# Moving the first two pairs' kv work, turns and numerator on the queues of a fused linear-attention and feed-forward kernel

## The chip, the cores and the metric

The kernel runs on one core of a Trainium2 chip. The metric is the device time of one execution in microseconds (us), median of three runs.

## The reference

A linear attention with a feature map, followed by a feed-forward layer with a leaky activation whose slope is learnt per column:

```python
def phi(x):                                   # x: [8, 8, 576, 64], w_phi: [64, 128]
    proj = np.einsum('bhsd,df->bhsf', x, w_phi)
    proj = proj - np.max(np.abs(proj), axis=-1, keepdims=True)
    return np.concatenate([np.exp(proj), np.exp(-proj)], axis=-1)
q_p, k_p = phi(q), phi(k)
kv  = np.einsum('bhsf,bhsd->bhfd', k_p, v)
z   = np.sum(k_p, axis=2)
num = np.einsum('bhsf,bhfd->bhsd', q_p, kv)
den = np.einsum('bhsf,bhf->bhs', q_p, z)[..., None] + 1e-06
x   = (num / den).transpose(0, 2, 1, 3).reshape(4608, 512)
h   = x @ w_in                                # w_in: [512, 2048]
g   = np.maximum(h, 0.0) + alpha * np.minimum(h, 0.0)
out = g @ w_out                               # w_out: [2048, 512]
```

## The kernel before

The attention runs over 32 pairs of heads (`NPAIR`, numbered from 0). For each pair these steps exist, each a small function in `attention_units(i)`:

- `load`, `load_v`: SyncE (SP) fetches k and q (tile `raw`, two buffers) and v.
- `project(0)` and `project(1)`: TensorE multiplies `raw` by `w_phi`. `project(0)` makes the four full k tiles (`pj`, 8 matmuls, the first burst); `project(1)` makes the last, half-filled k tile together with the last q tile (`pl`, 2 matmuls) and the four full q tiles (`pj`, 8 matmuls, the second burst). VectorE (DVE) then takes the largest absolute value (`m`, L320) and subtracts it (`t`, L321). From pair 2 on both bursts share one buffer of PSUM (`ps_pj`), so the second burst waits until DVE has read the first.
- `k_exp`: ScalarE (ACT) takes the two exponentials of the k tiles (`xk` for the four full ones, `k` for the last). The exponential of the last tile stands after the whole of `project(1)`, and waits until DVE has written all of its `t`.
- `k_z` (z, L374) and `k_acc` (kv, L357): matmuls into the tile `kv`, the z part first; the last quarter of each needs the `k` exponential. `kv_out` copies it (`ks`, ACT), `kv_turn` transposes it (`kt`, L389, TensorE), `kv_copy` copies that (`sf`, ACT).
- `q_turn` transposes the q tiles (`qt`, L400 and L403), `q_exp` takes their exponentials (`qf`, ACT); `den` and `num` (`d`, `n`) are the matmuls of denominator and numerator; then come the division by way of DRAM and the store of x.

Between these steps the weights of the feed-forward layer are unpacked in blocks of 256 columns: SP loads a block (`raww`), ACT scales it (`aw`, L176), DVE splits it in four instructions (L184 to L187), GpSimd (POOL) adds, ACT casts (`w`, L127), POOL subtracts. The first block is named `0_0`, the second `0_256`. `decode_at(t, blk)` gives each of these a place: for an early block the scale stands 0.25 ahead of the split.

The order on TensorE, ACT, DVE and SP is written by hand: every step is put in the list `todo` with a number, the pair's index plus its entry in `places(i)`, the list is sorted by it, and the engines get their instructions in that order. Each engine works its instructions off in order. PSUM tiles of the last tiles, of `kt`, of the third `qt`, of `d` and of `n` share three buffers (`ps_m`). The feed-forward matmuls start after some 108 us and fill the rest of the program.

Of the kernel before, what the change touches and what calls it, by code (L numbers as in the profile page):

```python
# [38 lines left out]
WA = (0.0040, 0.50)  # L39
# [19 lines left out]
def places(i):  # L59
    early = i < ZP  # L60
    end = i >= NPAIR - 2
    return dict(
        ld=-1.90,
        lv=-0.80,
        p=(-0.9955 if early else -0.993, 0.0),
        ke=(-0.26, 0.0011),
        ks=(0.0015, 0.0022, 0.0026),
        kz=1.0002,
        ka=1.0012,
        ko=1.0025,  # L70
        kr=1.10,
        kc=1.16,
        q=(1.34, 1.50, 1.20),
        qe=(1.46, 1.62, 1.28),
        d=2.0004,
        ds=2.0008,
        n=2.005,
        s=2.0055,
        d9=2.25,
        dv=3.0016 if early else 3.20 if end else 2.80,  # L80
        rd=3.0017 if early else 3.21 if end else 2.82,
        rr=3.20 if early else 3.45 if end else 3.001,
        x=3.45 if early else 3.60 if end else 3.20,
        xs=3.90 if early else 3.85 if end else 3.45,
    )


F0 = 9.23
# [24 lines left out]
def fused_kernel(ctx: ExitStack, tc: tile.TileContext, kq, v, w_phi, w_in, w_out, alpha, out):  # L113
# [110 lines left out]
    def decode_at(t, blk):  # L224
        return [(t + (WT if t < TL else WL)[k], lambda u=u: u(*blk, WN)) for k, u in stages.items()]
# [55 lines left out]
    def attention_units(i):  # L281
# [192 lines left out]
        def store():  # L474
            nc.sync.dma_start(x_d[hp, :, b * S : (b + 1) * S], c["s"])

        at = places(i)
        us = [
            (at["ld"], load),
# [143 lines left out]
    todo = []  # L623
# [6 lines left out]
    first = [(ff, z, o) for z in range(2) for ff in range(NF1) for o in range(0, 512, WN)]  # L630
# [1 line left out]
    late += [(ff, z) for z in (1, 0) for ff in range(NF1 + NA, NF - NL)]  # L632
    blocks = [(ff, z, o) for ff, z in late for o in range(0, 512, WN)]
    for n, blk in enumerate(first):
        todo += decode_at(1 + n // 2 + WA[n % 2], blk)
    for n, blk in enumerate(blocks):
        todo += decode_at(W2A + W2D * n, blk)
    todo += first_x()
# [179 lines left out]
```

## Time and profile before

| | |
|---|---|
| Median of three runs | 1132.7 us (1132.45 to 1134.01) |
| The profiled execution | 1133.75 us, of which 1132.0 us lie between its first and last instruction (its span) |
| Busy in the span: TensorE, DVE, ACT, POOL | 1115.9, 634.9, 560.8, 215.4 us |
| Chain that ended last, by engine | TensorE 90%, DVE 5%, ACT 2%, DMA 1%, issue 1%, POOL 1% |

All times of rows below are us from the start of the span. A row of the timeline gives the start and the length of a group of like instructions on one engine, then the line, the operation, what it writes and reads, and their number; in brackets stands idle time before it and what ended that. A matmul of 32-bit data appears as two records, so that a burst of 8 matmuls is "x16".

### The profile page before, as it was taken

The numbers are of one execution on the slowest core, as the hardware profiler recorded it, in microseconds if no ns is written. First come the engines' busy times: TensorE is split into PE (matmuls) and PEld (weight loads), VectorE is DVE, ScalarE is ACT, GpSimd is POOL, SyncE is SP. The second block draws the span as 40 slices with busy tenths as digits, with TensorE's granted clock in tenths as the row PEclk, the third lists the DMA queues.
The fourth block names the chain that finished last, engine by engine and source line by source line (L and its number), as shares of the span: only waits on it lengthen the run. The fifth ranks groups of instructions, "written<-read, shape, count | busy, mean of one in ns | idle before, by whom it ended". The sixth has DMA issues, their size and how long they took to land.

```text
span 1132.0 us, 18386 instructions
## 1 busy us (share of the span) xinstructions
PE 1115.9 (99%) x7246; PEld 868.6 (77%) x7246; DVE 634.9 (56%) x979; ACT 560.8 (50%) x1149; POOL 215.4 (19%) x219
## 2 busy tenths in 40 slices
PE   8999999999999999999999999999999999999998
PEld 6766777777777777677678888888888888888886
DVE  7888858698788777745862432424243423333323
ACT  5777665666676665664543342424333333333332
POOL 1345332423324242243542000000000000000000
PEclk9999999999999999999999999999999999999999
DMA  5466264546546364466616130303030302020021
GB/s 192 149 189 207 77 201 156 185 135 210 174 140 190 109 215 153 147 218 211 221 66 232 47 112 1 112 1 112 1 112 1 112 0 85 28 82 30 4 71 38
DMA packets 74245, 133.68 MB, mean 118 GB/s; under 512 B 14640, under 2 KB 24752, under 8 KB 73520
## 3 DMA queue, kind: packets, MB, share of 16 engines
q1 hardware_dynamic: 71856, 122.48, 33.5%
q0 software_dynamic: 2016, 9.96, 2.6%
q8 instruction: 57, 0.93, 0.3%
q14 instruction: 28, 0.23, 0.1%
q10 hardware_dynamic: 288, 0.07, 0.0%
HBM read 93.92 MB, written 38.42 MB: 117 GB/s over the span
## 4 chain that ended last, share of the span: by engine, by line
PE 90%; DVE 5%; ACT 2%; DMA 1%; issue 1%; POOL 1%; ACTq 0%; DVEq 0%; SPq 0%
PE h L512 11%; PE h L514 11%; PE h L513 11%; PE po L520 8%; PE po L518 8%; PE po L519 8%; PE kv L357 6%; PE pj L316 5%; PE n L422 5%; PE o L518 4%; PE o L520 4%; PE o L519 3%; PE d L440 2%; PE qt L403 2%; PE kv L374 1%; DVE m L320 1%
## 5 line engine op out<-in xcount | busy, mean ns | idle before, releaser
L243 DVE SCALAR_TENSOR_TENSOR g<-r,aln,g 128x512 f32<-128x512 f32 x144 | 112.8, 783 | 318.6 <-ACT g L239 318.2
L238 ACT ACTIVATE r<-h 128x512 f32<-128x512 f32 x144 | 86.7, 602 | 286.5 <-PE h L514 286.4
L131 DVE TENSOR_TENSOR gl<-g,gh 128x512 fp32r<-128x512 f32 x144 | 104.6, 726 | 84.8 <-ACT gh L127 84.3
L127 ACT CAST gh<-g 128x512 fp32r<-128x512 f32 x144 | 90.1, 626 | 94.3 <-DVE g L243 94.3
L239 ACT ACTIVATE g<-h 128x512 f32<-128x512 f32 x144 | 85.9, 597 | 2.5 <-DMA part_d<-os 2.5
L320 DVE TENSOR_REDUCE m<-pj 128x8 f32<-128x1024 f32 (+1 forms) x66 | 78.2, 1185 | 12.8 <-PE pj L316 12.6
L520 PE MATMUL po<-gl,wd 128*128 128x512 f32 x216 | 84.3, 390 | 0.0
L518 PE MATMUL po<-gh,wd 128*128 128x512 f32 x216 | 84.3, 390 | 0.0
L519 PE MATMUL po<-gh,wd 128*128 128x512 f32 x216 | 84.3, 390 | 0.0
L192 POOL TENSOR_TENSOR aw<-ew,aw 128x256 f32<-128x256 f32 x64 | 56.0, 875 | 129.4 <-DVE ew L187 127.9
L316 PE MATMUL pj<-w_sb,raw 64*128 64x128 f32 x1024 | 73.4, 283 | 7.0 <-DVE t L321 6.1
L316 PEld LDWEIGHTS pj<-w_sb,raw 64*128 64x128 f32 x1024 | 64.0, 191 | 21.0 <-issue 13.7
L321 DVE TENSOR_TENSOR t<-pj,m 128x1024 f32<-128x1024 f32 (+1 forms) x66 | 78.7, 1192 | 2.3
L518 PE MATMUL o<-gh,w 128*128 128x512 f32 x180 | 76.1, 423 | 0.2
L512 PE MATMUL h<-xh,w 128*128 128x512 f32 x180 | 75.8, 421 | 0.0
L472 POOL TENSOR_TENSOR s<-s,rr 128x576 f32<-128x576 f32 x32 | 48.1, 1502 | 143.9 <-DMA rr<-rec_d 111.0
L514 PE MATMUL h<-xl,w 128*128 128x512 f32 x180 | 70.9, 394 | 1.9 <-POOL xl L131 1.9
L520 PE MATMUL o<-gl,w 128*128 128x512 f32 x180 | 71.2, 396 | 1.5 <-DVE gl L131 1.3
L413 ACT ACTIVATE qf<-qt 128x512 f32<-128x512 f32 x128 | 68.5, 615 | 6.3 <-PE qt L403 6.3
L519 PE MATMUL o<-gh,w 128*128 128x512 f32 x180 | 70.6, 392 | 0.0
L513 PE MATMUL h<-xh,w 128*128 128x512 f32 x180 | 70.5, 392 | 0.0
L518 PE MATMUL po<-gh,w 128*128 128x512 f32 x180 | 70.2, 390 | 0.0
(108 smaller groups left out, 2409.4 us busy)
## 6 DMA issues: line engine op xcount, KB each, us to landing
xr<-x_d SPq DMA_DIRECT2D x18, 1024.0 KB
raw<-kq_dram SPq DMA_DIRECT2D x31, 576.0 KB
v<-v_dram SPq DMA_DIRECT2D x32, 320.0 KB
w_d<-raww SPq DMA_DIRECT2D x38, 256.0 KB
rr<-rec_d SPq DMA_DIRECT2D x64, 144.0 KB
x_d<-s SPq DMA_DIRECT2D x32, 288.0 KB
part_d<-os SPq DMA_DIRECT2D x36, 256.0 KB
pt<-part_d SPq DMA_DIRECT2D x9, 1024.0 KB
```

Of the source, the lines that this page charges most:

```text
L127: return act.copy(dst, src)
L131: return eng.tensor_tensor(dst, src, f(hi), op=ALU.subtract)
L238: act.activation(st["r"], ps, AF.Relu, scale=-1.0)
L243: dve.scalar_tensor_tensor(g, st["r"], aln[:, ff : ff + 1], g, op0=ALU.mult, op1=ALU.add)
L316: pe.matmul(dst[h, j], lhsT=c["raw"][hs, ts], rhs=w_sb[hs], start=True, stop=True)
L320: dve.tensor_reduce(m, src, axis=AX.X, op=ALU.max, apply_absolute_value=True)
L512: pe.matmul(ps, lhsT=wt[0][:, ws], rhs=xh, start=n == 0, stop=False)
L513: pe.matmul(ps, lhsT=wt[1][:, ws], rhs=xh, start=False, stop=False)
L514: pe.matmul(ps, lhsT=wt[0][:, ws], rhs=xl, start=False, stop=n == NK - 1)
L518: pe.matmul(ps, lhsT=wt[2][:, ws], rhs=gh, start=first, stop=False)
L519: pe.matmul(ps, lhsT=wt[3][:, ws], rhs=gh, start=False, stop=False)
L520: pe.matmul(ps, lhsT=wt[2][:, ws], rhs=gl, start=False, stop=last)
```

## The change

Three edits, all of them places in the order. Pair 0's z and kv matmuls, with the copy `ks`, move from behind pair 1's `project(1)` to ahead of it; pair 0's transposes and exponentials of q move ahead of pair 2's first burst; pair 0's numerator moves ahead of pair 3's first burst. Pair 1's z, kv and `ks` move ahead of pair 2's `project(1)`, z ahead of its first burst also. The unpacking of the first weight block moves ahead by 0.0044, which brings it from behind to ahead of pair 1's `project(1)`. No instruction is added or removed.

```diff
 def places(i):
     early = i < ZP
     end = i >= NPAIR - 2
+    first = {}
+    if i == 0:
+        first = dict(kz=0.9990, ka=0.9992, ko=0.9994, kr=1.0030, kc=1.0034, n=2.0041, q=(1.0032, 1.0033, 1.0031), qe=(1.0036, 1.0037, 1.0035))
+    if i == 1:
+        first = dict(kz=0.0044, ka=0.0046, ko=0.0048)
     return dict(
...
-    )
+    ) | first
...
     for n, blk in enumerate(first):
-        todo += decode_at(1 + n // 2 + WA[n % 2], blk)
+        todo += decode_at(1 + n // 2 + (WA[n % 2] if n else -0.0004), blk)
```

In the order below a name carries pair and part (`t_1_219` is the `t` of some pair's `project(1)`; the last number is that of the tile), and the lines of the changed kernel are 5 higher. The first place is DVE from pair 1's first burst on. Before, `pl_0_220` to `pj_1_222` are pair 1's `project(1)`, `aw_0_0` the first weight block and `pj_0_283` pair 2's first burst:

```order
L321 TENSOR_TENSOR t_0_189<-pj_0_1_191,m_0_1_203 128x512
L320 TENSOR_REDUCE m_1_0_233<-pl_0_220 128x1
L321 TENSOR_TENSOR t_1_219<-pl_0_220,m_1_0_233 128x128
L320 TENSOR_REDUCE m_1_1_236<-pl_1_221 128x1
L321 TENSOR_TENSOR t_1_219<-pl_1_221,m_1_1_236 128x128
L320 TENSOR_REDUCE m_1_2_239<-pj_1_222 128x8
L321 TENSOR_TENSOR t_1_219<-pj_1_222,m_1_2_239 128x2x512
L184 TENSOR_SCALAR aw_0_0_215<-aw_0_0_215 128x256
L185 SCALAR_TENSOR_TENSOR aw_0_0_215<-raww_0_0_210,aw_0_0_215 128x256
L186 TENSOR_SCALAR ew_0_0_277<-aw_0_0_215 128x256
L187 SCALAR_TENSOR_TENSOR ew_0_0_277<-raww_0_0_210,ew_0_0_277 128x256
L320 TENSOR_REDUCE m_0_0_292<-pj_0_283 128x8
```

The same place of the changed kernel:

```order
L326 TENSOR_TENSOR t_0_189<-pj_0_1_191,m_0_1_203 128x512
L189 TENSOR_SCALAR aw_0_0_215<-aw_0_0_215 128x256
L190 SCALAR_TENSOR_TENSOR aw_0_0_215<-raww_0_0_210,aw_0_0_215 128x256
L191 TENSOR_SCALAR ew_0_0_252<-aw_0_0_215 128x256
L192 SCALAR_TENSOR_TENSOR ew_0_0_252<-raww_0_0_210,ew_0_0_252 128x256
L325 TENSOR_REDUCE m_1_0_271<-pl_0_258 128x1
L326 TENSOR_TENSOR t_1_257<-pl_0_258,m_1_0_271 128x128
L325 TENSOR_REDUCE m_1_1_274<-pl_1_259 128x1
L326 TENSOR_TENSOR t_1_257<-pl_1_259,m_1_1_274 128x128
L325 TENSOR_REDUCE m_1_2_277<-pj_1_260 128x8
L326 TENSOR_TENSOR t_1_257<-pj_1_260,m_1_2_277 128x2x512
L325 TENSOR_REDUCE m_0_0_339<-pj_0_330 128x8
```

The four instructions of the first weight block now stand ahead of the six of pair 1's `project(1)`.

The second place is ACT from the `k` exponential of pair 1 (`k_1_132`) to the exponentials of pair 2's k tiles (`xk_339`). Before, where just ahead stand pair 1's `xk` and the scale of block `0_0`:

```order
L329 ACTIVATE k_1_132<-t_1_219 64x256 x2
L384 COPY ks_275<-kv_242 128x384
L393 COPY sf_302<-kt_295 128x384
L176 ACTIVATE aw_0_256_309<-raww_0_256_217 128x256
L411 ACTIVATE qf_311<-qt_2_304 128x2x64 x2
L127 CAST w_89<-aw_0_0_215 128x256
L413 ACTIVATE qf_311<-qt_0_316 128x512 x2
L413 ACTIVATE qf_311<-qt_1_324 128x512 x2
L334 ACTIVATE xk_339<-t_0_282 128x1024 x2
```

The same place of the changed kernel, with the same rows ahead:

```order
L389 COPY ks_250<-kv_219 128x384
L334 ACTIVATE k_1_132<-t_1_257 64x256 x2
L398 COPY sf_299<-kt_282 128x384
L416 ACTIVATE qf_301<-qt_2_286 128x2x64 x2
L418 ACTIVATE qf_301<-qt_0_289 128x512 x2
L418 ACTIVATE qf_301<-qt_1_294 128x512 x2
L389 COPY ks_352<-kv_308 128x384
L181 ACTIVATE aw_0_256_359<-raww_0_256_217 128x256
L132 CAST w_89<-aw_0_0_215 128x256
L339 ACTIVATE xk_372<-t_0_329 128x1024 x2
```

Pair 1's `ks` copy (`ks_352`) and, behind it, the scale of the second weight block (`aw_0_256`) now follow the whole of pair 0's q exponentials; before, that scale stood ahead of them, and pair 1's `ks` came later.

The third place is TensorE from pair 0's kv to pair 3's first burst (`raw_206` is pair 2's, `raw_299` pair 3's). Before, from the end of pair 0's q transposes:

```order
L403 MATMUL qt_1_324<-ident,t_1_164 128x128 x4
L316 MATMUL pl_0_348<-w_sb,raw_206 128x128
L316 MATMUL pl_1_349<-w_sb,raw_206 128x128
L316 MATMUL pj_1_350<-w_sb,raw_206 128x128 x8
L374 MATMUL kv_370<-xk_212,ones 32x128 x16
L374 MATMUL kv_370<-k_1_132,ones 32x128 x4
L440 MATMUL d_391<-qf_311,sf_302 32x288 x8
L357 MATMUL kv_370<-xk_212,v_208 64x256 x8
L357 MATMUL kv_370<-k_1_132,v_208 64x256 x2
L316 MATMUL pj_0_422<-w_sb,raw_299 128x128 x8
L422 MATMUL n_0_434<-qf_311,sf_302 64x288 x4
L422 MATMUL n_1_439<-qf_311,sf_302 64x288 x4
```

The changed kernel from the same point (`raw_354` is pair 3's):

```order
L379 MATMUL kv_308<-xk_212,ones 32x128 x16
L379 MATMUL kv_308<-k_1_132,ones 32x128 x4
L321 MATMUL pj_0_330<-w_sb,raw_206 128x128 x8
L362 MATMUL kv_308<-xk_212,v_208 64x256 x8
L362 MATMUL kv_308<-k_1_132,v_208 64x256 x2
L321 MATMUL pl_0_381<-w_sb,raw_206 128x128
L321 MATMUL pl_1_382<-w_sb,raw_206 128x128
L321 MATMUL pj_1_383<-w_sb,raw_206 128x128 x8
L445 MATMUL d_403<-qf_301,sf_299 32x288 x8
L427 MATMUL n_0_421<-qf_301,sf_299 64x288 x4
L427 MATMUL n_1_426<-qf_301,sf_299 64x288 x4
L321 MATMUL pj_0_432<-w_sb,raw_354 128x128 x8
```

Pair 1's z now stands ahead of pair 2's first burst, its kv between pair 2's two bursts, and pair 0's numerator ahead of pair 3's first burst instead of behind it. From pair 1's `kt` on all queues are in the old order.

## Rows read from the trace of the kernel before

**Rows 1.** Stretches: busy us (instructions) by engine, granted TensorE clock, DMA share, GB/s.
```profile
14.00:15.00 1.00, 1.00 (x18) 0.74 (x20) 0.97 (x2) 0.00 (x0) 0.00 (x0) 0.50 0.00 0
15.00:16.00 1.00, 1.00 (x26) 0.94 (x22) 0.93 (x5) 0.88 (x1) 0.00 (x0) 0.52 0.43 83
...
40.00:50.00 10.00, 10.00 (x137) 7.08 (x135) 8.62 (x18) 8.22 (x19) 4.28 (x5) 1.00 0.62 205
```

**Rows 2.** Chain that ended last, in order of time, around the first pairs.
```profile
21.20 1.24 DVE t L321
22.48 1.16 PE pj L316 x16
...
86.06 5.21 DMA raww<-w_out_dram
```

**Rows 3.** Timeline, TensorE: pair 1's second burst, pair 2's first, pair 1's kv, pair 3's bursts.
```profile
12.51 2.08 PE L316 MATMUL pj<-w_sb,raw 64*128 64x128 f32 x16 [2.08 <-DVE t L321]
...
18.73 1.16 PE L316 MATMUL pj<-w_sb,raw 64*128 64x128 f32 x16
...
25.77 1.95 PE L357 MATMUL kv<-xk,v 128*64 128x256 f32 x16
...
27.55 0.60 PE L357 MATMUL kv<-k,v 128*64 128x256 f32 x4
...
28.08 1.16 PE L316 MATMUL pj<-w_sb,raw 64*128 64x128 f32 x16
...
31.27 0.55 PE L389 MATMUL kt<-ident,ks 128*128 128x128 f32 x3
...
33.16 1.06 PE L316 MATMUL pj<-w_sb,raw 64*128 64x128 f32 x16
```

**Rows 4.** Timeline, ACT: exponentials of pairs 0 and 1, scale of the first block, pair 0's copy.
```profile
12.40 0.72 ACT L329 ACTIVATE k<-t 64x256 f32<-64x256 f32 x2 [1.43 <-DVE t L321]
...
15.12 2.01 ACT L334 ACTIVATE xk<-t 128x1024 f32<-128x1024 f32 x2 [2.00 <-DVE t L321]
...
17.03 0.42 ACT L176 ACTIVATE aw<-raww 128x256 f32<-128x256 f32 x1
...
18.56 0.72 ACT L329 ACTIVATE k<-t 64x256 f32<-64x256 f32 x2 [1.10 <-DVE t L321]
...
19.19 0.46 ACT L384 COPY ks<-kv 128x384 f32<-128x384 f32 x1
```

**Rows 5.** Timeline, DVE: pair 1's project(1), the first splits, bursts of pairs 2 and 3.
```profile
14.40 0.69 DVE L321 TENSOR_TENSOR t<-pj,m 128x512 f32<-128x512 f32 x1
...
15.00 0.28 DVE L320 TENSOR_REDUCE m<-pl 128x1 f32<-128x128 f32 x1
...
17.30 1.22 DVE L321 TENSOR_TENSOR t<-pj,m 128x1024 f32<-128x1024 f32 x1
...
18.44 0.28 DVE L184 TENSOR_SCALAR aw<-aw 128x256 uint32<-128x256 uint32 x1
...
19.55 0.42 DVE L187 SCALAR_TENSOR_TENSOR ew<-raww,ew 128x256 f32<-128x256 uint32 x1
...
22.34 0.46 DVE L184 TENSOR_SCALAR aw<-aw 128x256 uint32<-128x256 uint32 x1
...
26.34 1.22 DVE L321 TENSOR_TENSOR t<-pj,m 128x1024 f32<-128x1024 f32 x1
...
29.29 1.23 DVE L320 TENSOR_REDUCE m<-pj 128x8 f32<-128x1024 f32 x1 [0.20 <-PE pj L316]
...
30.55 1.23 DVE L321 TENSOR_TENSOR t<-pj,m 128x1024 f32<-128x1024 f32 x1
```

**Rows 6.** Timeline, TensorE's second bursts in three rounds around 86 us.
```profile
75.46 1.06 PE L316 MATMUL pj<-w_sb,raw 64*128 64x128 f32 x16
...
86.04 1.06 PE L316 MATMUL pj<-w_sb,raw 64*128 64x128 f32 x16
...
98.81 1.16 PE L316 MATMUL pj<-w_sb,raw 64*128 64x128 f32 x16 [1.04 <-DVE t L321]
```

## The prediction

> **What bounds the kernel now.** I read the stretches first. From 40 to 50 us TensorE is busy for the whole 10 us and DVE for 8.62 [rows 1], and so it goes on until some 86 us. The chain that ended last confirms it: from 22.48 on its pieces are TensorE's [rows 2], until a DMA at 86.06 [rows 2]. So nothing in this stretch wins time back: what the start-up loses or gains before TensorE is busy without a gap stays in the total, until 86 us at least. The question is only when TensorE reaches a point that both orders share. The first is pair 3's second burst at 33.16 [rows 3]: from the `kt` ahead of it all queues are alike, and both orders have done the same work by then.
>
> Ahead of that point TensorE does wait: 2.08 us before pair 1's second burst, ended by DVE's `t` [rows 3]. It also runs slowly for a time: the granted clock is 0.50 from 14 to 15 us and 0.52 from 15 to 16 [rows 1], which is the lower of its two levels, and the burst at 12.51 takes 2.08 us where the one at 18.73 takes 1.16 [rows 3]. This is what moving pair 0's z and kv into the gap can win. But the timelines of DVE and ACT show that both are queues in order that TensorE waits on, and the change moves rows on them too. So I follow the new order through the three queues.
>
> **The change, step by step.** No instruction is added or removed; durations stay as they are, only waits change. Up to DVE's `t` of pair 1's k tiles, which ends at 14.40 + 0.69 = 15.09 [rows 5], the queues of DVE and ACT are the old ones.
>
> *Step 1, the split of the first block waits.* DVE's next row is now this split instead of pair 1's `project(1)`. It needs ACT's scale, which stands behind pair 1's `xk` (15.12 + 2.01 = 17.13) and ends at 17.03 + 0.42 = 17.45 [rows 4]. DVE so idles from 15.09 to 17.48 (0.03 for the handover, as from 15.09 to ACT's 15.12 [rows 4]). Before, it worked on `project(1)` here, and the split came when the scale had long been done. The four instructions take 19.55 + 0.42 - 18.44 = 1.53 [rows 5], so until 19.02. Queued behind them are the six rows of pair 1's `project(1)`.
>
> *Step 2, pair 1's `project(1)` on DVE.* From the first `pl` to the end of the last `t` it took 17.30 + 1.22 - 15.00 = 3.52 [rows 5]. So its end is at 19.0 + 3.5 = 22.5, where it was 18.52: 4.0 us later. TensorE isn't what ends last here. Pair 0's z and kv wait for its `k` exponential (12.40 + 0.72 = 13.1 [rows 4]), then take the z rest of 0.2, kv 1.78 and 0.53 (starts of rows 25.77, 27.55 and 28.08 [rows 3]), then pair 1's `pl` and burst some 1.4: 17.1, or 18.5 if the clock is at half there. Both are before 20, when DVE first asks for that burst. So TensorE's own gain, 18.73 [rows 3] against 17.1, some 1.6 us, and the slow clock of [rows 1], both lie beside DVE's wait and are worth nothing.
>
> *Step 3, who waits for it.* ACT's pair 1 `k` exponential stands behind that `t` (0.72 [rows 4]): 22.54 to 23.26. Behind it on ACT are pair 0's `sf` and all its q exponentials. TensorE has done pair 0's `kt` and `qt` and pair 1's z but for its last quarter, which waits for this exponential; behind that wait stand pair 2's first burst and pair 1's kv. From 23.3: 0.2 of z, burst 1.09, kv 1.78 and 0.60 [rows 3], so kv ends at 26.95.
>
> *Step 4, the second block.* Pair 1's `ks` copy now stands ahead of the second block's scale on ACT, so that scale waits for kv too: 26.95 + 0.46 + 0.42 [rows 4] gives 27.8. DVE has done pair 2's first burst at 27.1 and waits again, since the second split is its next row. From that split to the end of pair 2's `t` DVE needed 26.34 + 1.22 - 22.34 = 5.22 without a gap [rows 5]: 27.85 + 5.22 = 33.1. TensorE meanwhile does pair 2's second burst and pair 0's `d` and `n`; pair 3's first burst waits for that `t` (one buffer of PSUM): 33.1 to 34.3.
>
> *Step 5, back on the common order.* DVE does the third block's split first, 33.0 to 34.55 (1.53 again), then `m` and `t` of pair 3's first burst, 30.55 + 1.23 - 29.29 = 2.49 [rows 5]: 37.0. TensorE needs only 33.16 - 31.27 = 1.89 [rows 3] from `kt` on and is ready at 36.1; before, the numerator stood between the bursts and covered this wait. Pair 3's second burst starts at 37.06 instead of 33.16: **+3.9 us**. Behind it DVE has the slack of [rows 1], some 1.4 us in 10, so the old rhythm is back within a round or two and the 3.9 us are handed on.
>
> SP's queue stands as before; pair 3's `raw` and the second pair of weight blocks are issued when pair 1's second burst has been read, some 2.5 to 4 us later than now, and are wanted only at 30 and 33. POOL's add and ACT's cast of the first blocks have no reader before the feed-forward part. I cost these at nothing; the cover is over 5 us.
>
> Sum: against the profiled execution, 1133.75 + 3.9 = 1137.6 (span 1132.0 + 3.9 = 1135.9). That execution is near the top of the three runs; on the median, 1132.7 + 3.9 = **1136.6 us**.
>
> Unknown costs. Handovers and the third split decide tenths: if the burst's end at 34.3 rather than the split sets step 5, it is 0.25 less, so 3.6. The clock is the larger one: new waits open on TensorE, and if the clock falls so that step 3's matmuls (z, burst, kv, 3.5 us together, which DVE and ACT wait for) run at half rate for as long as now from 12.51 to 16 [rows 1, 3], 3.5 us in which half the work is done, up to 1.7 us come on top. I take no fall at that place, since its waits are shorter than the 2.08 us that stands ahead of the fall now and lie between full stretches of work.
>
> **The rivals.**
>
> *A slow clock on the chain.* What speaks for it: step 3 comes after new waits on TensorE: `kt` waits from 17.1 for `ks` (17.45 + 0.46 [rows 4]), 0.8 us; the third `qt` for the buffer of pair 1's first `pl`, which DVE reads until 19.6, 1.3 us; z from 21.8 to 23.3, 1.5 us. And the trace shows a fall after less in sum (2.08 [rows 3], then 0.50 [rows 1]). Against: TensorE works over 2 us between them. It gives 3.9 + 1.7 = 5.6, 1138.3 us. The Trainium skill, "TensorE: Matmul & The Clock Gate", section "What's actually happening", bears on this: "the default state is throttled, and activity releases the throttle". By that rule a start-up with more waiting has the lower clock more often, and the sum would be this rival's; the trace agrees so far that the clock fell behind the wait and was back at 16 us, behind work without a gap.
>
> *The stall near 90 us gives it back: not slower.* The one place behind the start where TensorE is not the bound is 86.04 to 98.81, a round of 12.77 where the one before took 86.04 - 75.46 = 10.58 [rows 6]: 2.19 us of waits, which begin with a weight load issued at 86.06 that takes 5.21 to land [rows 2]. If those loads don't move with TensorE, the stall shrinks by up to 2.19: 1132.7 + 1.7 = 1134.4. It decides for "no change" once 1.7 of the 2.19 are gone. Against it: SP issues that load behind transfers that wait for ACT and TensorE of the same round, so it moves along.
>
> *The plan works as it reads: faster.* If DVE and ACT don't hold TensorE up, it reaches 17.1 instead of 18.73 with the same work done and keeps it: -1.6, 1131.1 us. That needs the first block's scale to be there by 15.1 and pair 1's `k` exponential not to wait, and in [rows 4] the scale can't start before `xk` ends at 17. That the change doesn't move what it says is excluded by the order itself.
>
> **How the numbers follow.** Forecast 0.72, slow clock 0.12, stall gives back 0.11, plan works 0.05. The prediction is the likeliest, 1136.6. The first two hold 0.84, so the range runs from the forecast's low end, 1132.7 + 3.6 less about half of the stall (1.1), so 1135.2, to the slow clock's 1138.3. 0.2% is 2.3 us, about what a measurement of this kernel can tell from no change. Slower: 0.72 + 0.12 = 0.84; same: 0.11; faster: 0.05.
>
> **What would show it.** In the changed profile: DVE idle of some 2.4 us at 15.1, ended by ACT's `aw`; the last `t` of pair 1 ending at 22.5; an idle time of over 4 us on ACT before pair 1's `k` exponential; TensorE waiting for ACT inside pair 1's z at 22 to 23; DVE waiting for `aw` near 27; pair 3's second burst at 37, and the second bursts after it 10.58 apart. The prediction is wrong if that burst stands below 35, or if the round at 86 (then 90) is shorter than 12.

## The result, and the profile after

The changed kernel takes 1138.1 us in the median of six runs (1136.59 to 1138.79). The kernel before, run beside it, takes 1134.31 us (1132.45 to 1135.46). The ratio is 1.0031 with a 95% interval of 1.0018 to 1.0043: slower, by 3.8 us. The profiled execution took 1137.18 us; its page, cut to the span, the busy times and the chain that ended last:

```profile
span 1135.4 us, 18387 instructions
...
PE 1115.9 (98%) x7246; PEld 866.9 (76%) x7246; DVE 638.9 (56%) x979; ACT 560.4 (49%) x1149; POOL 217.3 (19%) x219
...
PE 87%; DVE 6%; ACT 3%; DMA 2%; issue 1%; POOL 1%; DVEq 0%; ACTq 0%; SPq 0%
```

TensorE's work is the same 1115.9 us. The chain has lost 3 points on TensorE and won one each on DVE, ACT and DMA. Where that happened is seen in the stretch from 9 to 33 us, with one that reaches on to 46 us beside it (columns: length, then busy us and instructions of PE, PEld, DVE, ACT and POOL, granted TensorE clock, DMA share, GB/s). The kernel before:

```profile
9.00:46.00 37.00, 34.25 (x469) 25.82 (x473) 33.27 (x65) 25.94 (x58) 7.41 (x10) 0.95 0.47 158
9.00:33.00 24.00, 21.25 (x266) 16.07 (x268) 21.89 (x40) 15.36 (x34) 3.66 (x5) 0.93 0.51 175
```

The changed kernel, the same two stretches:

```profile
9.00:46.00 37.00, 30.30 (x389) 20.88 (x387) 29.91 (x53) 21.48 (x48) 6.84 (x9) 1.00 0.40 134
9.00:33.00 24.00, 18.01 (x230) 11.99 (x228) 17.86 (x32) 12.22 (x26) 3.19 (x4) 1.00 0.46 158
```

In this trace TensorE has the full clock in the whole stretch, where it had 0.93 before; that part of what the change can win is won here. But DVE works 17.86 of the 24 us where it worked 21.89: it stands still for 4 us more. The timeline of the changed kernel shows where (lines are 5 higher than before; in brackets the idle time ahead of a row and what ended it):

```profile
13.61 0.69 DVE L326 TENSOR_TENSOR t<-pj,m 128x512 f32<-128x512 f32 x1
...
15.36 1.06 PE L321 MATMUL pj<-w_sb,raw 64*128 64x128 f32 x16
...
16.24 0.41 ACT L181 ACTIVATE aw<-raww 128x256 f32<-128x256 f32 x1
...
16.69 0.29 DVE L189 TENSOR_SCALAR aw<-aw 128x256 uint32<-128x256 uint32 x1 [2.39 <-ACT aw L181]
...
17.80 0.43 DVE L192 SCALAR_TENSOR_TENSOR ew<-raww,ew 128x256 f32<-128x256 uint32 x1
...
18.14 0.28 DVE L325 TENSOR_REDUCE m<-pl 128x1 f32<-128x128 f32 x1
...
20.44 1.22 DVE L326 TENSOR_TENSOR t<-pj,m 128x1024 f32<-128x1024 f32 x1
...
21.69 0.72 ACT L334 ACTIVATE k<-t 64x256 f32<-64x256 f32 x2 [4.68 <-DVE t L326]
...
22.16 0.72 PE L379 MATMUL kv<-k,ones 128*32 128x128 f32 x8 [0.97 <-ACT k L334]
...
24.02 1.23 DVE L325 TENSOR_REDUCE m<-pj 128x8 f32<-128x1024 f32 x1 [2.37 <-PE pj L321]
...
27.24 0.29 DVE L189 TENSOR_SCALAR aw<-aw 128x256 uint32<-128x256 uint32 x1 [0.73 <-ACT aw L181]
...
27.58 1.01 POOL L136 TENSOR_TENSOR w<-aw,w 128x256 fp32r<-128x256 f32 x1 [8.54 <-ACT w L132]
...
28.03 0.71 DVE L191 TENSOR_SCALAR ew<-aw 128x256 uint32<-128x256 uint32 x1
...
29.95 2.16 PE L427 MATMUL n<-qf,sf 128*64 128x288 f32 x16 [1.02 <-DVE t L326]
...
31.49 1.23 DVE L326 TENSOR_TENSOR t<-pj,m 128x1024 f32<-128x1024 f32 x1
...
36.67 1.16 PE L321 MATMUL pj<-w_sb,raw 64*128 64x128 f32 x16 [0.71 <-DVE t L326]
```

The row of 16.69 is the one to see: DVE is free at 13.61 + 0.69 = 14.30 and waits 2.39 us for ACT's scale of the first weight block, with the six rows of pair 1's `project(1)` queued behind that wait. TensorE has had pair 1's second burst ready since 16.42, but DVE is through with it only at 21.66. Before, it was through at 18.52 [rows 5]. DVE waits twice more, 2.37 us at 24.02 for pair 2's first burst and 0.73 at 27.24 for the second block's scale. The chain that ended last (time, length, what) tells the same as one line of work that jumps between engines; from it:

```profile
14.33 2.00 ACT xk L339 x2
...
16.69 0.30 DVE aw L189
...
23.98 2.33 PE kv L362 x20
...
26.39 0.48 ACT ks L389
```

Pair 3's second burst, from which both orders are alike, starts at 36.67 instead of 33.16 [rows 3], 3.51 later, and the span is 1135.4 - 1132.0 = 3.4 longer. What lies behind that burst is 1135.4 - 36.67 = 1098.7 us now and 1132.0 - 33.16 = 1098.8 before: in these two traces nothing was given back.

**The measure for the experiments.** DVE's `t` of pair 1's k tiles ends at 14.30 in the changed kernel's trace and at 15.09 in that of the kernel before, and between 14.4 and 15.4 in those below. This difference stands from the first rows on: DVE's first `m`, ahead of all that the change moves, starts at 5.40 and at 6.19, behind a first burst of pair 0 of 1.16 and of 1.79 us. What lies behind pair 3's second burst is 1097.6 to 1100.7 us in the ten traces. Neither goes with the edits, and together they are as large as what is looked for. So each kernel is measured from the end of that `t` to the start of pair 3's second burst: 33.16 - 15.09 = 18.07 before, 36.67 - 14.30 = 22.37 now, a loss of 4.30. Between these marks DVE is busy for 16.18 us before and for 16.24 now, so that the loss is time in which DVE stands still. The medians of repeated runs stand beside it; their differences go with the measure within 0.8 us, but for ko1_back (1.7 against 3.1, which its interval takes in).

| kernel | measure, us | against before, us | median of runs, of before beside it | ratio, 95% |
|---|---|---|---|---|
| before | 18.07 | | | |
| changed | 22.37 | +4.30 | 1138.1, 1134.31 | 1.0018 to 1.0043 |
| split_only | 22.60 | +4.53 | 1138.55, 1133.32 | 1.0022 to 1.0055 |
| split_back | 19.83 | +1.76 | 1135.6, 1133.32 | 0.9990 to 1.0025 |
| scale_early | 19.91 | +1.84 | 1135.42, 1134.32 | 0.9999 to 1.0027 |
| ko1_back | 21.15 | +3.08 | 1136.06, 1134.32 | 1.0012 to 1.0043 |
| sb_ko1_back | 18.57 | +0.50 | 1134.5, 1134.32 | 0.9990 to 1.0017 |
| n_back | 25.43 | +7.36 | 1141.05, 1133.32 | 1.0045 to 1.0080 |
| cast_late | 21.97 | +3.90 | 1138.32 (one run), 1134.32 | |
| z0early | 18.01 | -0.06 | 1133.43, 1133.32 | 0.9980 to 1.0015 |

### The profile page after: what moved, and what is told of

Same layout as the page of the kernel before. It is cut to its first block, busy times and chain, and to the rows that moved or that the text cites. A ratio compares the mean times of both kernels' runs of the same rounds, so it can differ in the third digit from the quotient of the medians.

```text
span 1135.4 us, 18387 instructions
## 1 busy us (share of the span) xinstructions
PE 1115.9 (98%) x7246; PEld 866.9 (76%) x7246; DVE 638.9 (56%) x979; ACT 560.4 (49%) x1149; POOL 217.3 (19%) x219
## 4 chain that ended last, share of the span: by engine, by line
PE 87%; DVE 6%; ACT 3%; DMA 2%; issue 1%; POOL 1%; DVEq 0%; ACTq 0%; SPq 0%
PE h L517 11%; PE h L519 10%; PE h L518 10%; PE po L523 7%; PE po L525 7%; PE po L524 7%; PE kv L362 5%; PE pj L321 5%; PE n L427 5%; PE o L523 4%; PE o L525 4%; PE o L524 3%; PE d L445 2%; PE qt L408 2%; DVE m L325 1%; PE kv L379 1%
## 5 line engine op out<-in xcount | busy, mean ns | idle before, releaser
L136 DVE TENSOR_TENSOR gl<-g,gh 128x512 fp32r<-128x512 f32 x144 | 104.6, 726 | 84.8 <-ACT gh L132 84.3
```

What stands on the lines that cost most here:

```text
L136: return eng.tensor_tensor(dst, src, f(hi), op=ALU.subtract)
```

## The experiments

The theory is that of the prediction: two waits of DVE for ACT's scale, each with the next pair's work queued behind it. The rivals are a slow clock on the chain, and that the new order of TensorE itself costs the time.

### The first block's move alone, and all but it

split_only is the kernel before with nothing but this line:

```diff
-        todo += decode_at(1 + n // 2 + WA[n % 2], blk)
+        todo += decode_at(1 + n // 2 + (WA[n % 2] if n else -0.0004), blk)
```

> The kernel before with one of the three edits alone: the first weight block's place moves by 0.0044, so that DVE's four split instructions stand ahead of pair 1's project(1); all matmuls stay where they were. Measure: from the end of DVE's t of pair 1's k tiles to the start of pair 3's second burst (18.07 us in the kernel before, 22.37 in the changed one). Theory Q (queues: the split row held by ACT's scale delays DVE, and all else hangs on that): 21.8 us, some 3.8 over before in the total, and a single wait of about 5.5 us on TensorE ahead of pair 2's first burst. Rival T (the moved matmuls cost it: numerator, kv, turns): 18.1 us, total as before within 0.3.

Timeline of split_only, DVE and TensorE:

```profile
17.76 0.29 DVE L184 TENSOR_SCALAR aw<-aw 128x256 uint32<-128x256 uint32 x1 [2.39 <-ACT aw L176]
...
21.51 1.22 DVE L321 TENSOR_TENSOR t<-pj,m 128x1024 f32<-128x1024 f32 x1
...
22.84 1.22 PE L316 MATMUL pj<-w_sb,raw 64*128 64x128 f32 x16 [3.79 <-issue]
...
24.00 0.89 PE L389 MATMUL kt<-ident,ks 128*128 128x128 f32 x3
...
37.97 1.06 PE L316 MATMUL pj<-w_sb,raw 64*128 64x128 f32 x16
```

DVE's wait is the same 2.39 us, and here TensorE shows it in one place: 3.79 us ahead of pair 2's first burst. That is less than the 5.5 expected; pair 0's kv ahead of it ends only at 18.45 + 0.60 = 19.05. The profile names no releaser ("issue"), but DVE's `t`, which reads the buffer that this burst fills, ended at 21.51 + 1.22 = 22.73. The measure is 0.8 above what was expected. That part is the clock: behind the 3.79 us in which TensorE did nothing it is granted at half from 24 to 27 us,

```profile
25.00:26.00 1.00, 1.00 (x7) 1.00 (x6) 0.97 (x2) 1.00 (x5) 0.00 (x0) 0.50 0.00 0
```

and `kt` takes 0.89 instead of 0.55 [rows 3]; pair 2's second burst starts at 27.39, where DVE's `t` would have let it start at 26.62. So the one edit, without any of the others, costs as much as the whole change, 0.77 of it by way of the clock, which did not fall in the changed kernel's trace.

split_back is the changed kernel with that line as it was before.

> The changed kernel with that one edit undone: the first weight block stands where it was, all moved matmuls and copies stay moved. Theory Q: 19.0 us on the same measure (1.0 over before; up to 2.7 over before if TensorE's clock is at half from 12.5 to 16 or later on the path), total some 1 to 2.7 over before; no wait on DVE for the scale at 15. Rival T: 22.4 us, total as the changed kernel, some 3.9 over before.

Two waits of DVE in split_back, whose `t` ends at 14.70, and pair 3's second burst:

```profile
15.97 0.29 DVE L325 TENSOR_REDUCE m<-pl 128x1 f32<-128x128 f32 x1 [1.27 <-PE pl L321]
...
25.09 0.29 DVE L189 TENSOR_SCALAR aw<-aw 128x256 uint32<-128x256 uint32 x1 [0.74 <-ACT aw L181]
...
34.53 1.16 PE L321 MATMUL pj<-w_sb,raw 64*128 64x128 f32 x16 [0.71 <-DVE t L326]
```

The loss falls from 4.30 to 1.76. That is 0.8 more than expected, and not by the clock, which is 1.00 from one mark to the other: the second wait stays, 0.74 at 25.09, which is taken up below. The two prices, 4.53 alone and 1.76 for the rest, don't add up to 4.30. Of the 4.53, 0.77 are the clock; and the 1.27 us for which DVE waits here at 15.97, since pair 0's kv now stands ahead of pair 1's `pl` on TensorE, lie in the changed kernel beside the wait for the scale: 4.53 + 1.76 - 0.77 - 1.27 = 4.25.

### Is it the place or the wait?

scale_early leaves the split where the change puts it, and moves ACT's scale of that block ahead of pair 1's `xk`, so that the split finds it done:

```diff
-        return [(t + (WT if t < TL else WL)[k], lambda u=u: u(*blk, WN)) for k, u in stages.items()]
+        early = dict(scale=-0.28) if blk == (0, 0, 0) else {}
+        return [(t + ((WT if t < TL else WL) | early)[k], lambda u=u: u(*blk, WN)) for k, u in stages.items()]
```

> The changed kernel with the scale of the first weight block put ahead of pair 1's xk on ACT; DVE's split keeps its new place ahead of pair 1's project(1). It takes away what makes the split wait, not the split's place. Theory Q: DVE starts the split at the end of pair 1's k tiles, and pair 1's t is done 5.1 us after that instead of 7.4; pair 3's second burst follows 19.9 us after that end instead of 22.4, total 2.4 under the changed kernel. Rival (the place of the four instructions costs it, held or not): 1.5 us of them stay on the path, 21.5 to 22.4, total as changed.

Timeline of scale_early, ACT, DVE, TensorE (lines behind the added one are one higher here):

```profile
13.62 0.44 ACT L181 ACTIVATE aw<-raww 128x256 f32<-128x256 f32 x1 [0.81 <-DMA raww<-w_in_dram]
...
14.70 0.28 DVE L189 TENSOR_SCALAR aw<-aw 128x256 uint32<-128x256 uint32 x1
...
34.69 1.16 PE L322 MATMUL pj<-w_sb,raw 64*128 64x128 f32 x16 [0.71 <-DVE t L327]
```

DVE takes the split without a gap, and the measure falls by 2.46, about the 2.39 us of the wait, to the value of split_back. The place of the split on DVE costs nothing that can be seen here; that ACT's scale isn't done when DVE comes to it is what costs. Here means beside the moved matmuls: the split fills the 1.27 us for which DVE waits in split_back. What the place would cost with TensorE's old order was not run.

### The second wait

In ko1_back pair 1's `ks` copy goes back to its old place, behind the second block's scale and pair 2's exponentials of k on ACT; sb_ko1_back does that and puts the first block back too.

```diff
-        first = dict(kz=0.0044, ka=0.0046, ko=0.0048)
+        first = dict(kz=0.0044, ka=0.0046)
```

> The changed kernel with pair 1's ks copy put back behind the second block's scale on ACT; the rest as changed. It isolates step 4 of the forecast, the wait of DVE for that scale near 27. Theory Q: that wait of 0.7 goes, 21.6 us on the same measure, total 0.8 under the changed kernel. Rival (DVE is held there by its own queue anyway): 22.4, no change.

> The changed kernel with both undone: the first block's split and pair 1's ks copy are where they were, the moved matmuls of both pairs stay. Theory Q: only the uncovered order of the bursts is left, 18.2 to 18.7 us on the same measure (18.07 before), total as before within 0.6, with TensorE's gap ahead of pair 1's second burst filled and nothing won by it. Rival T (matmuls cost it): above 20. Rival P (filled gap pays): 16.5 to 17.

ko1_back, DVE's third instruction of the second block and pair 3's second burst:

```profile
27.48 0.29 DVE L191 TENSOR_SCALAR ew<-aw 128x256 uint32<-128x256 uint32 x1
...
35.71 1.16 PE L321 MATMUL pj<-w_sb,raw 64*128 64x128 f32 x16 [0.67 <-DVE t L326]
```

and the same burst of sb_ko1_back, whose `t` ends at 14.44:

```profile
33.01 1.16 PE L321 MATMUL pj<-w_sb,raw 64*128 64x128 f32 x16 [0.67 <-DVE t L326]
```

ko1_back is 1.22 better than the changed kernel: the wait of 0.73 at 27.24 is gone, and so are 0.42 of the third instruction, of which more below. With both undone only 0.50 of the 4.30 are left, and the time can't be told from the kernel before (1.0004). So the two waits of DVE for ACT, and what hangs on them, are the loss; what all other moves cost together, gains and losses set off, is half a microsecond. The single steps agree: 4.30 less 2.46 (scale_early) less 1.22 leaves 0.62. Among what makes up this rest, with what the moves win set against it, is the wait of 2.37 us at 24.02. It doesn't hang on the first wait: scale_early has it at the same length (22.03). Pair 2's first burst stands behind pair 1's z now, and so behind the `k` exponential, and the split no longer lies between it and pair 1's `t` on DVE.

### The numerator

n_back is the changed kernel with pair 0's numerator in its old place, behind pair 3's first burst (`n=2.0041` taken out of pair 0's places).

> The changed kernel with pair 0's numerator put back behind pair 3's first burst; the rest as changed. In my forecast the numerator ahead of that burst uncovered a wait of 0.9 us at pair 3's second burst. Theory Q: the numerator now fills the wait for DVE's t of pair 2, which only opens with it gone, so putting it back makes it worse: a wait of some 3.7 us ahead of pair 3's first burst, 23.1 us on the same measure, 1.2 over the changed kernel. Rival T: the wait at the second burst is covered again and 0.9 comes back, 21.5 us.

Timeline of n_back, TensorE, and the stretch from 35 to 36 us:

```profile
34.11 1.98 PE L321 MATMUL pj<-w_sb,raw 64*128 64x128 f32 x16 [3.89 <-issue]
...
36.02 2.96 PE L427 MATMUL n<-qf,sf 128*64 128x288 f32 x16
...
40.80 1.06 PE L321 MATMUL pj<-w_sb,raw 64*128 64x128 f32 x16
```

```profile
35.00:36.00 1.00, 1.00 (x11) 0.79 (x8) 0.50 (x2) 0.00 (x0) 0.39 (x1) 0.50 0.46 176
```

The wait ahead of pair 3's first burst is 3.89 us, close to the 3.7 expected. The measure is 2.3 above the 23.1 expected (the 1.2 given beside it would make 23.6), and most of that is the rival of the slow clock: behind the wait the burst takes 1.98 instead of 1.16 and the numerator 2.96 instead of 2.16 (the burst at full clock as in [rows 3], the numerator as in the changed kernel at 29.95), 1.6 us together. The numerator's move is thus the part of the change that earns something, 25.43 - 22.37 = 3.06 us with those 1.6 in it, but only against a wait that the other parts make: before, pair 3's first burst at 28.08 had none [rows 3].

### The size of the loss

cast_late takes from the changed kernel only the overlap at 28.03: ACT's cast and GpSimd's subtraction (L136) of the first block come later.

```diff
+        late = dict(high=0.80, low=0.85) if blk == (0, 0, 0) else {}
```

> The changed kernel with ACT's cast of the first weight block put behind pair 2's xk, so that GpSimd's subtraction of that block no longer runs beside DVE's split of the second block. In the changed kernel the third instruction of that split takes 0.71 us beside that subtraction, and the subtraction 1.01. If the overlap makes both long: 0.29 and 0.73, and 22.0 us on the same measure instead of 22.4. If the place in the split makes it long: 0.71 stays.

```profile
28.52 0.29 DVE L191 TENSOR_SCALAR ew<-aw 128x256 uint32<-128x256 uint32 x1
...
36.75 1.16 PE L322 MATMUL pj<-w_sb,raw 64*128 64x128 f32 x16 [0.71 <-DVE t L327]
```

In this timeline of cast_late DVE's instruction is back from 0.71 to 0.29 and the measure is 21.97, 0.40 lower, so this overlap is the 0.40 by which the loss exceeds the forecast. GpSimd's side is shorter too: its two subtractions of L136 take 1.41 us together (30.28), where the one at 27.58 took 1.01. The time of the one run, 1138.32, can't show 0.4 us; the trace alone does.

### What the gap of the kernel before was worth

z0early is the kernel before with 16 of pair 0's z matmuls, those that don't need the `k` exponential, ahead of pair 1's `project(1)`. Together with the `pl` matmuls, which now stand behind them, they fill most of the 2.08 us ahead of its second burst [rows 3].

```diff
-            (at["kz"], k_z),
+            *([(at["kz"], k_z)] if i >= NZ else [(at["kz0"], lambda: k_z(0)), (at["kz"], lambda: k_z(1))]),
```

> The kernel before with the 16 z matmuls of pair 0 that need only the four full k tiles put into the gap of 2.08 us ahead of pair 1's project(1); nothing else moves, on no other engine. Theory Q: TensorE starts pair 1's second burst no later, but pair 2's first burst still waits for DVE's t of pair 1, so the filled gap comes back there as a wait of some 2.5 us: 18.0 us on the same measure, total as before within 0.3. Rival P (the gap is TensorE's to win, so filling it pays): 1.0 to 1.7 us less than before.

Timeline of z0early, and two of its stretches:

```profile
12.78 1.16 PE L321 MATMUL pj<-w_sb,raw 64*128 64x128 f32 x16
...
17.57 1.22 DVE L326 TENSOR_TENSOR t<-pj,m 128x1024 f32<-128x1024 f32 x1
...
18.90 1.16 PE L321 MATMUL pj<-w_sb,raw 64*128 64x128 f32 x16 [2.29 <-issue]
```

```profile
14.00:15.00 1.00, 1.00 (x16) 0.59 (x14) 0.97 (x3) 0.00 (x0) 0.00 (x0) 1.00 0.18 34
9.00:33.00 24.00, 20.29 (x264) 14.67 (x264) 21.90 (x41) 15.18 (x33) 3.65 (x5) 1.00 0.53 180
```

The gap is filled and the clock is full, where it was 0.50 from 14 to 15 us [rows 1]. What TensorE so gains comes out as 2.29 us of waiting ahead of pair 2's first burst, until DVE's `t` ends at 18.79. The measure is 18.01, that of the kernel before, and DVE is busy 21.90 of the 24 us, as before (21.89). Up to pair 2's first burst the start-up is bound by DVE, and TensorE's gap and slow clock there were worth nothing.

## Why the prediction was right

The direction, the place and the steps held, the time lies inside the range. Times below are counted from the end of DVE's `t` of pair 1's k tiles, forecast against measured:

| step | forecast | changed kernel |
|---|---|---|
| 1: DVE waits for the first scale | 2.39 | 2.39 |
| 1: the split's four instructions | 1.53 | 17.80 + 0.43 - 16.69 = 1.54 |
| 2: pair 1's `project(1)` on DVE | 3.52 | 20.44 + 1.22 - 18.14 = 3.52 |
| 3: pair 1's kv ends | 26.95 - 15.09 = 11.86 | 23.98 + 2.33 - 14.30 = 12.01 |
| 4: second split begins | 27.85 - 15.09 = 12.76 | 27.24 - 14.30 = 12.94 |
| 4: second split to pair 2's `t` | 5.22 | 31.49 + 1.23 - 27.24 = 5.48 |
| 5: from there to pair 3's second burst | 37.06 - 33.1 = 3.96 | 36.67 - 32.72 = 3.95 |

Step 1 to 3 are right to tenths, for a plain reason: the durations stay, so that one has only to play the queues by hand. **The mis-sized term is step 4's**, 0.26 too small, with handovers of 0.18 ahead of it. The 5.22 were taken from a stretch where GpSimd met DVE once too, but shorter: there the split's first row took 0.46 [rows 5] where 0.28 is usual. In the changed kernel the second block's split falls beside GpSimd's subtraction, and its third instruction takes 0.71. I had counted the rows on each queue and not asked which rows of two engines would now run at the same time. Without that meeting (cast_late) the stretch takes 5.05: the forecast's 0.17 for the shorter meeting and its missing handovers cancel, which is why cast_late has the forecast's 21.97 to the digit.

**The level.** 1136.6 was forecast and 1138.1 measured, near the top of the range. The 1.5 us are the base: 1132.7 was the median of three runs, and six runs give 1134.31. The difference, 3.9 forecast, is 3.8. That the time still lies inside the range is in part luck: the top of the range, 1138.3, was the price of the slow clock, which this trace does not have, and it happened to cover the error of the base.

**The rivals.** The slow clock did not come in the trace of the changed kernel: it has 1.00 from 9 to 46 us, although TensorE waited for `ks`, for `qt` and inside z as the rival said. It came in n_back, and not only behind the wait of 3.89: the granted clock is at half there from 21 to 24 us too, behind waits of 0.74 and 1.22 us for `ks` and `qt` which the changed kernel has as well,

```profile
22.00:23.00 1.00, 1.00 (x28) 0.92 (x24) 0.74 (x1) 0.23 (x1) 0.00 (x0) 0.50 0.79 305
```

so that another execution of the changed kernel could show it, at a price of some 0.2 us there: from DVE's `t` to pair 2's first burst it is 24.11 - 22.74 = 1.37 us in n_back and 22.82 - 21.66 = 1.16 in the changed kernel. The 1.7 of the rival were a bound. Whole executions say a little more: the mean granted clock is 0.994 to 0.997 in the ten of split_only, 0.995 to 0.997 in the eight of n_back and 0.998 to 1.000 in the six of the changed kernel. The falls of the first two are thus hardly an accident of one trace; whether some execution of the changed kernel had a short one in the start-up is open. By the rule of the Trainium skill that the prediction set beside this rival ("TensorE: Matmul & The Clock Gate", "What's actually happening") more waiting has the lower clock more often; n_back agrees, and the changed kernel, with more waiting and 1.00 against 0.95 from 9 to 46 us, does not. The stall near 90 us gave nothing back, as the second bursts of the rounds show:

```profile
79.08 1.06 PE L321 MATMUL pj<-w_sb,raw 64*128 64x128 f32 x16
...
89.66 1.06 PE L321 MATMUL pj<-w_sb,raw 64*128 64x128 f32 x16
...
102.28 1.16 PE L321 MATMUL pj<-w_sb,raw 64*128 64x128 f32 x16 [0.18 <-DVE t L326]
```

One round takes 10.58, as before, and the one with the stall 12.62, where it took 12.77 [rows 6]. The plan as it reads is answered by z0early and sb_ko1_back: with TensorE's gap filled, and then with all the moved matmuls and neither wait for a scale, the measure is 18.01 and 18.57. Pair 2's first burst waits for DVE's `t`, so that bringing TensorE forward ahead of it wins nothing.

**What stays open.** The 0.50 that sb_ko1_back still loses, the sum of what the moved matmuls, turns and copies win and cost, is not taken apart here. The order that keeps the split's new place and cures both waits at once, scale_early with ko1_back, was not run either; by the sum above, an estimate, it would lose some 0.6. No order that was run is below 18.0 on the measure, so none of them beats the kernel before.

## What to carry to other kernels

Before filling a gap on one engine, look who ends last on the other side of it: here DVE was busy for 21.9 of 24 us, and TensorE's gap only lay beside that work. When a row is moved forward on an in-order queue, follow what it needs to its own queue: the split moved by six rows, its scale on ACT did not move past `xk`, and all that stood behind the split paid the difference. And play all moved queues on one clock, with an eye to which engines' rows will newly run side by side.

## What the runs showed of the hardware

Not expected was that DVE and GpSimd hold each other up. A DVE `TENSOR_SCALAR` on 128x256 uint32 takes 0.29 us alone. When it comes while a GpSimd subtraction is running, it ends 0.15 behind the end of that, wherever in it the DVE instruction began: 28.74 against 28.59 in the changed kernel, 27.32 against 27.17 in split_only, where it took 0.82. In the kernel before:

```profile
33.38 0.74 POOL L131 TENSOR_TENSOR w<-aw,w 128x256 fp32r<-128x256 f32 x1 [3.49 <-ACT w L127]
...
33.64 0.63 DVE L186 TENSOR_SCALAR ew<-aw 128x256 uint32<-128x256 uint32 x1
```

33.64 + 0.63 = 34.27, and 33.38 + 0.74 = 34.12. The Trainium skill, "SBUF — State Buffer", section "Who interferes with whom", has a rule for this: the two engines share a pair of ports, a DVE `tensor_scalar` in a two-port mode wants it whole, and whoever issues first keeps it for its whole instruction. DVE's side agrees. GpSimd's is less clear: its subtraction took 1.01 where it began 0.01 behind a two-input instruction of DVE (27.57) and 0.74 where it began 0.28 behind one, and why isn't shown.

The other surprise is how little a half clock can matter. In the kernel before it lay from 14 to 16 us beside DVE's work and cost nothing, as z0early shows; in n_back it lay on the chain and cost 1.6 us.
